# First eight chunks in fp32 on the Sync queue, a hand-ordered prologue, and a rearranged attention step in a fused retention and squared-ReLU kernel

## The chip, the cores and the metric

One core of one Trainium2 chip. The metric is the device time of one execution in microseconds (us). Runs of a kernel are compared with runs of the kernel before on the same chip. Two executions, one in run 8 and one in run 9, were marked slow (over 1.5% above the fastest of the same kernel); medians and ranges below leave them out.

Engine names follow the profile: PE is TensorE (matmul), PEld its weight loads, DVE is VectorE, ACT is ScalarE, POOL is GpSimd, SP is Sync. A name ending in q is that engine's sequencer.

## The reference

```python
# q, k, v: (4, 8, 768, 64) fp32;  w_in: (512, 2048);  w_out: (2048, 512)
gamma = 1 - 2.0 ** (-5 - arange(8));  scale = 1 / sqrt(64)
for t in range(768):
    state = gamma * state + outer(k[t], v[t])       # for each batch and head
    y[t] = scale * q[t] @ state
x = y.transpose(0, 2, 1, 3).reshape(3072, 512)
h = maximum(x @ w_in, 0)
out = (h * h) @ w_out                               # (3072, 512) fp32
```

The kernel cuts the 3072 tokens into 24 chunks of 128 tokens, six to a batch. For each chunk, the attention part scales k, transposes k and q, forms scores under a causal mask, and adds what the running state gives. The feed-forward part (`f1`, `f2`) then runs on blocks of chunks. All matmuls are bf16.

## The kernel before

Parts that the change and the argument touch; `...` marks cuts.

```python
blocks = [[0, 1], [2, 3]]            # then four chunks each
def load_chunk(m):                   # k in fp32 on Sync; q and v cast to bf16 on the way, on POOL
    for name, src, dt in (("kn", k, FP32), ("qs", q, BF16), ("vs", v, BF16)):
        t = ldpool.tile([P, H, D], dt, tag=name, name=f"{name}{m}")
        eng = nc.sync if dt == FP32 else nc.gpsimd
        eng.dma_start(t[:], src[b, :, i * C : (i + 1) * C, :].rearrange("h s d -> s h d"))
def load_w(which, s): ...            # a quarter of w_in or w_out, cast to bf16, on POOL

load_chunk(0)
... # identity, on POOL
load_chunk(1)
... # the constants for the decay factors, on POOL: iota ex_i, causal mask, iota t_i
load_chunk(2); load_chunk(3)
for s in range(NSL): load_w("i", s)

def a_cast(m):  # DVE: ks = k * factor
def a_turn(m):  # PE: 8 transposes;  ACT: PSUM -> kqT
def a_score(m): # PE: 8 matmuls of 64 rows (row tiles);  DVE: mask -> pt
def a_out(m):
    ...
    if i > 0:
        for p in range(NP):
            for hh in range(2):
                r = slice(64 * hh, 64 * hh + 64)
                nc.tensor.matmul(yt[r, p, :], lhsT=s_bf[r, p, :], rhs=kqT[r, 1, p, :], ...)  # 64x64 tiles
    ... # 8 value matmuls (64-column tiles), 8 matmuls for the state c (64-column tiles)
    ... # DVE: xts = yt * yf;  ACT: state copy c -> s
def f1(b, fb):  # 4 matmuls, ACT relu, DVE square
def f2(b, j, part): # 4 matmuls; after the last part ACT copies and Sync stores

a_cast(0); a_turn(0); fill_yf(0, C)
a_cast(1); a_turn(1); a_score(0); fill_yf(C, S)
...
# f1(0) with chunks 2 and 3 between, f1(1), f2(0), f2(1); then each block woven with the
# attention pieces of the next: a_score, a_cast, a_turn and a_out, each a piece of its own
```

Of the kernel before, what the change touches and what calls it, by code (L numbers as in the profile page):

```python
# [18 lines left out]
def kernel(  # L19
# [9 lines left out]
    nc = tc.nc  # L29
# [11 lines left out]
    assert NCB == NP and S % C == 0 and NFB % 4 == 0  # L41
    NSL = 4
    FPS = NFB // NSL
    FW = FPS * P
    scale = 1.0 / float(np.sqrt(D))
    gammas = [1.0 - 2.0 ** (-5.0 - h) for h in range(H)]

    blocks = [[0, 1], [2, 3]]
    while blocks[-1][-1] + 1 < NCHUNK:
        c0 = blocks[-1][-1] + 1  # L50
        blocks.append(list(range(c0, min(c0 + 4, NCHUNK))))
    where = {m: (b, j) for b, ms in enumerate(blocks) for j, m in enumerate(ms)}
# [4 lines left out]
    ldpool = ctx.enter_context(tc.tile_pool(name="ldpool", bufs=7))  # L57
    bfpool = ctx.enter_context(tc.tile_pool(name="bfpool", bufs=4))
    atpool = ctx.enter_context(tc.tile_pool(name="atpool", bufs=3))
    xtpool = ctx.enter_context(tc.tile_pool(name="xtpool", bufs=3))  # L60
    hpool = ctx.enter_context(tc.tile_pool(name="hpool", bufs=2))
# [11 lines left out]
    raw = {}  # L73
    w_in_bf = [const.tile([P, NCB, FW], BF16, name=f"w_in_bf{s}") for s in range(NSL)]
    w_out_bf = [const.tile([P, FPS, DM], BF16, name=f"w_out_bf{s}") for s in range(NSL)]

    def load_chunk(m):
        b, i = divmod(m, NCH)
        got = []
        for name, src, dt in (("kn", k, FP32), ("qs", q, BF16), ("vs", v, BF16)):  # L80
            t = ldpool.tile([P, H, D], dt, tag=name, name=f"{name}{m}")
            eng = nc.sync if dt == FP32 else nc.gpsimd
            eng.dma_start(  # L83
                t[:], src[b, :, i * C : (i + 1) * C, :].rearrange("h s d -> s h d")
            )
            got.append(t)
        raw[m] = got

    def load_w(which, s):
        if which == "i":  # L90
            nc.gpsimd.dma_start(w_in_bf[s][:], w_in_v[:, :, s * FW : (s + 1) * FW])
        else:
            nc.gpsimd.dma_start(w_out_bf[s][:], w_out_v[:, s * FPS : (s + 1) * FPS, :])

    load_chunk(0)


    ident = const.tile([P, P], BF16)
# [10 lines left out]
    load_chunk(1)  # L109

    lng = const.tile([P, H], FP32)
    for h in range(H):
        nc.gpsimd.memset(lng[:, h : h + 1], float(np.log(gammas[h])))
    ex_i = const.tile([P, NCH, H], I32)
    nc.gpsimd.iota(ex_i[:], pattern=[[C, NCH], [0, H]], base=0, channel_multiplier=1)
# [11 lines left out]
    lnp = const.tile([P, NP], FP32)  # L127
    for h in range(H):
        r = slice(64 * (h % 2), 64 * (h % 2) + 64)
        nc.gpsimd.memset(lnp[r, h // 2 : h // 2 + 1], float(np.log(gammas[h])))  # L130
    t_i = const.tile([P, S], I32)
    nc.gpsimd.iota(t_i[:], pattern=[[1, S]], base=0, channel_multiplier=0)

    load_chunk(2)
    load_chunk(3)
    for s in range(NSL):
        load_w("i", s)


    ex_f = const.tile([P, NCH, H], FP32)  # L140
    nc.vector.tensor_copy(ex_f[:], ex_i[:])
    nc.vector.tensor_tensor(
        out=ex_f[:],
        in0=ex_f[:],
# [5 lines left out]
    nc.vector.tensor_scalar_mul(kf[:], kf[:], scale)  # L150
# [3 lines left out]
    yf = const.tile([P, NP, S], FP32)  # L154

    def fill_yf(lo, hi):
        for p in range(NP):
            nc.scalar.activation(  # L158
                yf[:, p, lo:hi], t_f[:, lo:hi], AF.Exp, scale=lnp[:, p : p + 1]
            )  # L160

# [5 lines left out]
    def a_cast(m):  # L167
        i = m % NCH
        kn, qs, vs = raw.pop(m)
        ks = bfpool.tile([P, H, D], BF16, tag="ks", name=f"ks{m}")  # L170
        nc.vector.tensor_tensor(  # L171
            out=ks[:],
            in0=kn[:],
            in1=kf[:, i, :, None].to_broadcast([P, H, D]),
            op=ALU.mult,
        )
        at[m] = dict(ks=ks, qs=qs, vs=vs)

    def a_turn(m):
        a = at[m]  # L180
        tp = ps_tp.tile([P, 2, NP, P], BF16, tag="tp", name=f"tp{m}")
        for j, src in enumerate((a["ks"], a["qs"])):
            for p in range(NP):
                nc.tensor.transpose(tp[:, j, p, :], src[:, 2 * p : 2 * p + 2, :], ident[:])  # L184
        kqT = atpool.tile([P, 2, NP, P], BF16, tag="kqT", name=f"kqT{m}")
        nc.scalar.activation(kqT[:], tp[:], AF.Copy)
        a["kqT"] = kqT
# [24 lines left out]
    def a_out(m):  # L212
        i = m % NCH
        a = at.pop(m)
        ks, vs, kqT, pt = a["ks"], a["vs"], a["kqT"], a["pt"]
        b, j = where[m]
        if j == 0:
            xts[b] = xtpool.tile([P, NP, 4 * P], BF16, tag="xt", name=f"xt{b}")
        yt = ps_yt.tile([P, NP, P], FP32, tag="yt", name=f"yt{m}")
        if i > 0:  # L220
            s_bf = state["s"]
            for p in range(NP):
                for hh in range(2):
                    r = slice(64 * hh, 64 * hh + 64)
                    nc.tensor.matmul(
                        yt[r, p, :],
                        lhsT=s_bf[r, p, :],
                        rhs=kqT[r, 1, p, :],
                        start=(p == 0),
                        stop=False,  # L230
                        skip_group_check=True,
                    )
        for p in range(NP):
            for hh in range(2):
                r = slice(64 * hh, 64 * hh + 64)
                nc.tensor.matmul(
                    yt[r, p, :],
                    lhsT=vs[:, 2 * p + hh, :],
                    rhs=pt[:, hh, p, :],
                    start=(i == 0 and p == 0),  # L240
                    stop=(p == NP - 1),
                    skip_group_check=True,
                )
        if i < NCH - 1:
# [3 lines left out]
            for p in range(NP):  # L248
                for hh in range(2):
                    h = 2 * p + hh  # L250
                    r = slice(64 * hh, 64 * hh + 64)
                    nc.tensor.matmul(  # L252
                        c[r, p, :],
                        lhsT=ks[:, h, :],
                        rhs=vs[:, h, :],
                        start=(i == 0 and p == 0),
                        stop=(p == NP - 1),
                        skip_group_check=True,
                    )
        nc.vector.tensor_tensor(  # L260
            out=xts[b][:, :, j * P : (j + 1) * P],
            in0=yt[:],
            in1=yf[:, :, i * C : (i + 1) * C],
            op=ALU.mult,
        )
        if i < NCH - 1:
            s_new = atpool.tile([P, NP, D], BF16, tag="s", name=f"s{m}")
            nc.scalar.activation(s_new[:], c[:], AF.Copy)
            state["s"] = s_new
# [4 lines left out]
    def f1(b, fb):  # L274
        n = len(blocks[b]) * P
        if fb == 0:
            h2s[b] = hpool.tile([P, NFB, 4 * P], BF16, tag="h2", name=f"h2_{b}")
        h2 = h2s[b]
        hp = ps_f.tile([P, 4 * P], FP32, tag="psf", name=f"hp{b}_{fb}")
        s, r = divmod(fb, FPS)  # L280
        for cb in range(NCB):
# [3 lines left out]
                rhs=xts[b][:, cb, :n],  # L285
# [3 lines left out]
        nc.scalar.activation(h2[:, fb, :n], hp[:, :n], AF.Relu)  # L289
        nc.vector.tensor_mul(h2[:, fb, :n], h2[:, fb, :n], h2[:, fb, :n])  # L290
# [3 lines left out]
    def f2(b, j, part):  # L294
        m = blocks[b][j]
# [3 lines left out]
        for r in range(FPS):  # L299
# [3 lines left out]
                lhsT=h2s[b][:, fb, j * P : (j + 1) * P],  # L303
# [8 lines left out]

    def all_f1(b):
        return [lambda fb=fb: f1(b, fb) for fb in range(NFB)]

    def all_f2(b):
        return [
            lambda j=j, s=s: f2(b, j, s) for j in range(len(blocks[b])) for s in range(NSL)
        ]

    def stages(ms):

        seq = []
        for n in range(len(ms) + 2):
            if 0 <= n - 1 < len(ms):
                seq.append(lambda m=ms[n - 1]: a_score(m))
            if n < len(ms):
                seq.append(lambda m=ms[n]: a_cast(m))
                seq.append(lambda m=ms[n]: a_turn(m))
            if 0 <= n - 2 < len(ms):  # L330
                seq.append(lambda m=ms[n - 2]: a_out(m))
        return seq

    def weave(quanta, side):
        n, done = len(quanta), 0
# [6 lines left out]


    a_cast(0)
    a_turn(0)
    fill_yf(0, C)
    a_cast(1)
    a_turn(1)
    a_score(0)
    fill_yf(C, S)  # L350
    a_cast(2)
    a_turn(2)
    a_out(0)
    a_score(1)
    a_out(1)
    a_cast(3)
    a_score(2)
    a_turn(3)
    load_chunk(4)
    load_w("o", 0)  # L360
    load_chunk(5)
    load_w("o", 1)
    load_chunk(6)
    load_w("o", 2)
    load_chunk(7)
    load_w("o", 3)
    load_chunk(8)

    q0 = all_f1(0)
    side = [lambda: a_out(2), lambda: a_score(3), lambda: a_out(3)]  # L370
    for fb in range(NFB):
        q0[fb]()
        if fb in (1, 3, 6):
            side.pop(0)()
    nxt = 9
    q1 = all_f1(1)
    for x in range(NFB // 2):
        q1[x]()
    weave(q1[NFB // 2 :] + all_f2(0) + all_f2(1), stages(blocks[2]))
    for b in range(2, len(blocks)):  # L380
        while nxt < NCHUNK and nxt <= blocks[b][-1] + 5:
            load_chunk(nxt)
            nxt += 1
        weave(all_f1(b) + all_f2(b), stages(blocks[b + 1]) if b + 1 < len(blocks) else [])
# [30 lines left out]
```

## Time and profile before

| | before |
|---|---|
| median of its first 3 runs | 239.28 us (238.09 to 240.16) |
| profiled run, its span | 237.42 us, 235.7 us |
| PE busy | 214.2 us, 91% |
| first transposes / first feed-forward matmul | 9.55 / 22.68 us |
| block of four chunks in the middle | 34.95 us |
| last block, without attention | 27.66 us |

The Trainium skill ("Trainium Kernel Development and Optimization", Performance Expectations) warns that matmul busy time is a bad measure of distance to the roofline. The argument here therefore goes by starts: the time from the start of one group of matmuls to the start of the next is what that group costs PE.

The page, busy times (us, share of the span, instructions), and two rows of its 40 slices:

```profile
PE 214.2 (91%) x1728; PEld 110.9 (47%) x1728; DVE 101.4 (43%) x188; ACT 109.6 (46%) x190; POOL 51.5 (22%) x82
...
PE   0166997799999999999999999999999999999993
...
PEclk9999999999999999999999999999999999999999
```

PE is full from the fifth slice on, but for a dip near 40 us. The loss is at the start. The view of waits of PE from 0 to 65 us (what waited, for what, us in total, times, longest) tells why:

```profile
PE tp_172 L184 <- DVE ks_170 L171: 9.6, 1, 9.6
PE tp_217 L184 <- DVE ks_215 L171: 1.9, 1, 1.9
...
PE tp_646 L184 <- DVE ks_637 L171: 1.0, 1, 1.0
PE tp_594 L184 <- DVE ks_585 L171: 1.0, 1, 1.0
PE hp_0_348 L282 <- DMA w_in_bf_93<-in_moe_w_in_dram: 0.7, 1, 0.7
...
PE st_612 L196 <- ACT kqT_603 L186: 0.7, 1, 0.7
```

PE stood 9.6 us for the first scaled k. Its data had landed at about 3.5 us. What was missing were the factors, whose first input, `ex_i`, POOL made only after issuing four loads. This is POOL's timeline (start, us, engine, line, operation, out<-in, count):

```profile
1.27 1.01 POOL L83 DMA_DIRECT2D qs_103<-in_q_dram  x1 [0.80 <-POOLq L399]
...
3.69 0.89 POOL L83 DMA_DIRECT2D qs_114<-in_q_dram  x1
...
5.73 0.21 POOL L115 IOTA ex_i<- 128x48 int32 x1
...
11.97 0.79 POOL L91 DMA_DIRECT2D w_in_bf_93<-in_moe_w_in_dram  x1
```

PE's timeline near the first feed-forward, whose groups of four are `hp`:

```profile
22.68 1.03 PE L282 MATMUL hp_0_348<-xt_228,w_in_bf_93 128*128 128x256 bf16 x4 [0.71 <-DMA w_in_bf_93<-in_moe_w_in_dram]
23.51 1.06 PE L282 MATMUL hp_1_355<-xt_228,w_in_bf_93 128*128 128x256 bf16 x4
...
27.11 0.61 PE L282 MATMUL hp_4_416<-xt_228,w_in_bf_94 128*128 128x256 bf16 x4
27.55 0.60 PE L282 MATMUL hp_5_423<-xt_228,w_in_bf_94 128*128 128x256 bf16 x4
```

From 22.68 to 23.51 a group of four takes 0.83 us; from 27.11 to 27.55 the same shape takes 0.44. PE is slow ("cold") until it has been busy for a while, as the Trainium skill ("TensorE: Matmul & The Clock Gate", Part 1) describes. The row PEclk, the clock granted by the throttle, does not show this: the trace's first clock record begins at 25.67 us, and the row counts time without a record as full. The starts show it.

In the middle of the kernel, PE's timeline reads so (`tp` transposes, `st` scores, `yt` L225 state product, `yt` L236 values, `c` the new state):

```profile
105.61 1.03 PE L282 MATMUL hp_6_1422<-xt_1104,w_in_bf_94 128*128 128x512 bf16 x4
106.66 0.40 PE L184 MATMUL tp_1429<-ident,ks_1413 128*128 128x128 bf16 x4
...
107.98 1.03 PE L282 MATMUL hp_8_1447<-xt_1104,w_in_bf_95 128*128 128x512 bf16 x4
108.94 0.40 PE L196 MATMUL st_1454<-kqT_1438 64*128 64x128 bf16 x8
109.27 1.04 PE L282 MATMUL hp_9_1465<-xt_1104,w_in_bf_95 128*128 128x512 bf16 x4
...
127.41 1.03 PE L301 MATMUL op_1641<-w_out_bf_99,h_3_1355 128*128 128x512 bf16 x4
128.37 0.41 PE L225 MATMUL yt_1665<-kqT_1504,s_1632 64*64 64x128 bf16 x8
128.71 0.41 PE L236 MATMUL yt_1665<-pt_1563,vs_1339 128*64 128x128 bf16 x8
128.96 0.29 PE L252 MATMUL c_1530<-vs_1339,ks_1479 128*64 128x64 bf16 x8
129.18 1.04 PE L301 MATMUL op_1641<-w_out_bf_100,h_3_1355 128*128 128x512 bf16 x4
```

The column after the operands tells the part of the array that a matmul uses: 128\*128 is all of it, 64\*128 a row tile, 128\*64 a column tile, 64\*64 both. These are called forms below. A feed-forward group of four takes 0.86 us by itself. It takes 0.96 in front of a score (107.98 to 108.94) or a state product (127.41 to 128.37): entering the tiled form costs 0.10 us. It takes 1.05 in front of these transposes (105.61 to 106.66). No PE wait over the listing's threshold is reported there, but the waits of the weight loads show one:

```profile
PEld L184 <- DVE ks_1413 L171: 0.5, 1, 0.5
```

DVE ended the scaling of that k at 106.61, 0.05 us before the load. Six of the last twelve chunks lose 0.19 us in this way, the other six nothing.

### The profile page before, as it was taken

What the parts mean: (1) busy time and instruction counts of PE and PEld (TensorE: products, weight loads), DVE (VectorE), ACT (ScalarE), POOL (GpSimd) and SP (SyncE); (2) the same over time, 40 slices, a digit from 0 to 9 for tenths busy, and PEclk for the clock granted to TensorE, in tenths of its full rate; (3) what the DMA queues carried; (4) which work ended last, traced back from release to release, by engine and by line L of the source; (5) the groups of instructions that cost most, each with busy time, mean ns of one, the idle gap of its engine ahead of it and who ended that gap; (6) DMA issues with size and microseconds to landing.
All of it is one profiled execution on the core that took longest, in us unless ns stands there. A gap on an engine that the chain in (4) does not pass through costs nothing.

```text
span 235.7 us, 4145 instructions
## 1 busy us (share of the span) xinstructions
PE 214.2 (91%) x1728; PEld 110.9 (47%) x1728; DVE 101.4 (43%) x188; ACT 109.6 (46%) x190; POOL 51.5 (22%) x82
## 2 busy tenths in 40 slices
PE   0166997799999999999999999999999999999993
PEld 0145785454544444444445544444544554444441
DVE  0446665642356533356634266534266524144100
ACT  2292586432277721277722277621377622277221
POOL 8983155642410102410203410100000000000000
PEclk9999999999999999999999999999999999999999
DMA  8999999998994087993078992041170011100112
GB/s 130 215 191 197 198 181 190 185 161 127 138 183 79 3 89 87 111 185 65 4 88 91 112 194 54 2 64 47 46 178 4 0 47 46 63 29 0 42 47 89
DMA packets 82579, 23.34 MB, mean 99 GB/s; under 512 B 75392, under 2 KB 79488, under 8 KB 82560
## 3 DMA queue, kind: packets, MB, share of 16 engines
q0 software_dynamic: 54144, 10.49, 52.7%
q1 hardware_dynamic: 28416, 12.59, 20.3%
q8 instruction: 13, 0.21, 0.4%
q14 instruction: 6, 0.05, 0.1%
HBM read 27.26 MB, written 6.29 MB: 142 GB/s over the span
## 4 chain that ended last, share of the span: by engine, by line
PE 85%; DMA 5%; POOL 4%; DVE 2%; ACT 1%; issue 1%; ACTq 0%; POOLq 0%
DMA w_in_bf_93<-in_moe_w_in_dram 5%; PE op_2057 L301 2%; PE op_1641 L301 2%; PE op_1232 L301 2%; PE op_865 L301 2%; PE op_795 L301 2%; PE op_2470 L301 2%; PE op_2411 L301 2%; PE op_762 L301 2%; PE op_2378 L301 2%; PE op_1549 L301 2%; PE op_1140 L301 2%; PE op_2529 L301 2%; PE op_2008 L301 2%; PE op_1975 L301 2%; PE op_1700 L301 2%
## 5 line engine op out<-in xcount | busy, mean ns | idle before, releaser
L282 PEld LDWEIGHTS <-w_in_bf_93 128*128 128x128 bf16 x112 | 10.6, 101 | 9.6 <-DMA w_in_bf_93<-in_moe_w_in_dram 1.0
L282 PEld LDWEIGHTS <-w_in_bf_95 128*128 128x128 bf16 x112 | 10.5, 98 | 9.3
L282 PEld LDWEIGHTS <-w_in_bf_94 128*128 128x128 bf16 x112 | 10.6, 98 | 8.9
L282 PEld LDWEIGHTS <-w_in_bf_96 128*128 128x128 bf16 x112 | 10.3, 98 | 8.2
L290 DVE TENSOR_TENSOR h_6_2567<-h_6_2567 128x512 bf16<-128x512 bf16 x16 | 6.8, 426 | 10.1 <-ACT h_6_2567 L289 10.1
L290 DVE TENSOR_TENSOR h_5_2177<-h_5_2177 128x512 bf16<-128x512 bf16 x16 | 6.8, 424 | 9.4 <-ACT h_5_2177 L289 9.4
L290 DVE TENSOR_TENSOR h_4_1774<-h_4_1774 128x512 bf16<-128x512 bf16 x16 | 6.8, 424 | 9.4 <-ACT h_4_1774 L289 9.4
L290 DVE TENSOR_TENSOR h_2_939<-h_2_939 128x512 bf16<-128x512 bf16 x16 | 6.8, 423 | 9.4 <-ACT h_2_939 L289 9.4
L290 DVE TENSOR_TENSOR h_3_1355<-h_3_1355 128x512 bf16<-128x512 bf16 x16 | 6.8, 424 | 8.9 <-ACT h_3_1355 L289 8.9
L301 PEld LDWEIGHTS <-h_6_2567 128*128 128x128 bf16 x64 | 6.3, 98 | 7.5
L184 PE MATMUL tp_172<-ident,ks_170 128*128 128x128 bf16 x4 | 0.6, 307 | 9.6 <-DVE ks_170 L171 9.6
L301 PEld LDWEIGHTS <-h_4_1774 128*128 128x128 bf16 x64 | 5.8, 98 | 6.5
L301 PEld LDWEIGHTS <-h_2_939 128*128 128x128 bf16 x64 | 5.8, 98 | 6.5
L301 PEld LDWEIGHTS <-h_5_2177 128*128 128x128 bf16 x64 | 5.8, 98 | 6.5
L301 PEld LDWEIGHTS <-h_3_1355 128*128 128x128 bf16 x64 | 5.8, 98 | 6.5
L290 DVE TENSOR_TENSOR h_1_528<-h_1_528 128x256 bf16<-128x256 bf16 x16 | 4.6, 291 | 4.8 <-ACT h_1_528 L289 3.7
L290 DVE TENSOR_TENSOR h_0_347<-h_0_347 128x256 bf16<-128x256 bf16 x16 | 4.5, 291 | 4.8 <-ACT h_0_347 L289 3.5
L184 PEld LDWEIGHTS <-ks_170 128*128 128x128 bf16 x4 | 0.3, 130 | 9.5 <-DVE ks_170 L171 9.5
L301 PEld LDWEIGHTS <-h_1_528 128*128 128x128 bf16 x32 | 2.8, 98 | 3.1
L158 ACT ACTIVATE yf<-t_f,lnp 128x128 f32<-128x128 f32 (+1 forms) x8 | 4.2, 603 | 0.0
L301 PEld LDWEIGHTS <-h_0_347 128*128 128x128 bf16 x32 | 2.9, 98 | 2.8
L83 POOL DMA_DIRECT2D vs_2173<-in_v_dram x1 | 0.9, 876 | 13.9 <-PE c_1530 L252 13.9
(803 smaller groups left out, 516.5 us busy)
## 6 DMA issues: line engine op xcount, KB each, us to landing
w_in_bf_93<-in_moe_w_in_dram POOLq DMA_DIRECT2D x1, 512.0 KB, 10.7
w_in_bf_94<-in_moe_w_in_dram POOLq DMA_DIRECT2D x1, 512.0 KB, 13.2
w_in_bf_95<-in_moe_w_in_dram POOLq DMA_DIRECT2D x1, 512.0 KB, 15.2
w_in_bf_96<-in_moe_w_in_dram POOLq DMA_DIRECT2D x1, 512.0 KB, 17.1
w_out_bf_97<-in_moe_w_out_dram POOLq DMA_DIRECT2D x1, 512.0 KB, 17.6
w_out_bf_98<-in_moe_w_out_dram POOLq DMA_DIRECT2D x1, 512.0 KB, 13.7
w_out_bf_99<-in_moe_w_out_dram POOLq DMA_DIRECT2D x1, 512.0 KB, 11.8
w_out_bf_100<-in_moe_w_out_dram POOLq DMA_DIRECT2D x1, 512.0 KB, 11.6
```

The costliest lines, as they stand in the source:

```text
L83: eng.dma_start(t[:], src[b, :, i * C : (i + 1) * C, :].rearrange("h s d -> s h d"))
L158: nc.scalar.activation(yf[:, p, lo:hi], t_f[:, lo:hi], AF.Exp, scale=lnp[:, p : p + 1])
L184: nc.tensor.transpose(tp[:, j, p, :], src[:, 2 * p : 2 * p + 2, :], ident[:])
L282: nc.tensor.matmul(hp[:, :n], lhsT=w_in_bf[s][:, cb, r * P : (r + 1) * P], rhs=xts[b][:, cb, :n], start=(cb == 0), stop=(cb == NCB - 1),)
L290: nc.vector.tensor_mul(h2[:, fb, :n], h2[:, fb, :n], h2[:, fb, :n])
L301: nc.tensor.matmul(op[:], lhsT=h2s[b][:, fb, j * P : (j + 1) * P], rhs=w_out_bf[part][:, r, :], start=(fb == 0), stop=(fb == NFB - 1),)
```

## The change

The change's intent: the first eight chunks of q and v come in fp32 on one Sync queue and are cast by engines; the weights are issued between chunks 0 to 3 and chunks 4 to 7; POOL makes constants first; dummy matmuls keep PE warm; the first blocks are ordered by hand; the state product becomes four full-array matmuls on block-diagonal tiles; and the score of the next chunk stands directly behind the value and state matmuls.

```diff
-    blocks = [[0, 1], [2, 3]]  # then fours
+    for n in (2, 2, 1, 3, 4, 4, 4, 4): ...
+    FIRST = 8                                  # fp32 on Sync for q, v of chunks below 8
+    for m in range(4):
+        load(nc.sync, "k", m); load(nc.sync, "q", m); load(nc.sync, "v", m)
     ... # POOL: the two iotas, identity and mask now come before any DMA issue; small memsets on DVE
 def a_cast(m):
-        nc.vector.tensor_tensor(out=ks[:], in0=kn[:], in1=kf..., op=ALU.mult)
+        nc.vector.scalar_tensor_tensor(out=ks[:], in0=kn.pop(m)[:], scalar=scale, in1=kf..., ...)
+        if m < FIRST:
+            if m < 4: nc.scalar.activation(qs[m][:], qn.pop(m)[:], AF.Copy)
+            else:     nc.gpsimd.tensor_copy(qs[m][:], qn.pop(m)[:])
+            nc.gpsimd.tensor_copy(vs[m][:], vn.pop(m)[:])
 def a_out(m, after=None):
-                for hh in range(2): nc.tensor.matmul(yt[r, p, :], lhsT=s_bf[r, p, :], rhs=kqT[r, 1, p, :], ...)
+                nc.tensor.matmul(yt[:, p, :], lhsT=s_bd[i % 2][:, p, :], rhs=kqT[:, 1, p, :], ...)
-            nc.scalar.activation(s_new[:], c[:], AF.Copy)
+            for hh in range(2): nc.scalar.activation(s_bd[(i + 1) % 2][r, :, r], c[r, :, :], AF.Copy)
+        if after is not None: a_score(after)
+def fill(n): # n matmuls of zeros, 512 columns
+run("Y0 Z12 K0 T0 Y1 Z2 K1 S0 Z2 T1 P0 K2 S1 Y2 Z2 T2")     # K cast, T turn, S score, P out,
+load_w_in(0); load_w_in(1)                                   # Y fill_yf, Z fill, F f1, G f2, L load
+run("P1 K3 S2 Y3 Z2 T3 P2 S3 Y4 Z4")
+... # w_in 2, 3; w_out 0..3; chunks 4..7 on Sync, the first behind the landing of w_out 2
+run("F0.0 P3 Y5 F0.1 F0.2 F0.3 F1.0 F1.1 F1.2 F1.3")
+... # then f1 and f2 of chunks 0..3 weight slice by weight slice
+run("K4 G0.3 G1.3 G2.3 K5 T4 G3.0 S4 G3.1 T5 G3.2 P4 S5 G3.3 K6")
+... # block of chunk 4 alone, then chunks 5..7, then fours
+def side(ms): # for each chunk: a_turn(m + 1); cast(m + 2); a_out(m, m + 1)
```

## The prediction

> **What bounds it now.** By the page, TensorE (PE) is 91% busy and 85% of the chain that ended last. From block 2's first matmul (timeline: 64.6 us) to the last block's (204.4) PE never waits: 34.95 us per block of four chunks. The last block, without attention woven in, takes 27.66, so attention costs (34.95 - 27.66)/4 = 1.82 us per chunk. After it come 3.6 us of eviction, store. Of the first 64.6 us, four chunks of feed-forward (27.7 us) and eight of attention (14.6) would fill 42.3; some 22 are lost:
> - PE waits 9.6 us for the first scaled k (waits view); k landed at 3.6, but its factors came from POOL behind four DMA issues (the iota only at 5.73).
> - chunk 3's v lands at 19.4; weights start behind it in the same POOL queue, at half the packets' share; w_in 0 lands at 22.6.
> - PE is slow until about 25.8: four 256-column matmuls take 0.85 us at 22.7 and 0.44 from 27.1. It is the warm-up the Trainium skill ("TensorE: Matmul & The Clock Gate", Part 1) describes; the trace agrees.
> - from 35 to 45 us PE idles 2.9 us, on k scaling and PSUM evictions.
>
> **The change.**
> 1. Twelve fp32 loads on Sync. Alone, 256-byte packets ran at about 920 per us (packet records, 172 to 175 us), so 1.12 us for a tensor: k0 3.6, q0 4.7, v2 12.5, v3 16. That is no more bandwidth (cast loads reach 1,190 packets per us); what is gained is order.
> 2. POOL makes constants first; kf ready near 2.7 us. First transposes at 5.5 rather than 9.55, after dummy matmuls that should warm PE by then.
> 3. w_in 0 and 1 issue after v2's cast (13.4), so w_in 0's packets meet nearly no competition: first packet 16, at 192 per us 2.7 us, landed 20.4; the other slices every 2.7 us, w_out 3 at 39. Attention for chunks 0 to 2 is then done. PE takes 3.5 us a slice over four chunks, slower than slices land, so never waits.
> 4. Loads of chunks 4 to 7 wait for w_out 2 (36.4) and land from 39 to 51, ahead of use.
> 5. Steady state: four full-array state matmuls (about 0.23 us) replace eight tiled ones (0.34); score directly behind value and key-value products saves one mode entry, 0.10 us (feed-forward quartet 0.86 alone, 0.96 before a tiled group). About 0.2 us per chunk.
> 6. Added: casts on ACT and POOL, two state copies rather than one, a one-chunk block whose evictions are tight. 1 to 2 us of stalls.
>
> **Sum.** First feed-forward 2.3 us earlier; the remaining attention moved before it 1.3; warm start 1.9; stalls near 40 us 3; steady state 3.5; minus 1.5 to 2. About 10 us: span near 225.7, time **229.5 us** (225.5 to 233.5). Faster by over 2%: 0.92; same 0.07; slower 0.01.
>
> **Right or wrong.** Right: first feed-forward matmul at 20 to 21 us at full speed; no PE wait over 1 us after; the full blocks at about 34.2 us rather than 34.95; same tail. Wrong: weights landing after 22; PE cold at 20; block period unchanged.
>
> **What could upset it.** POOL casts slow enough to hold the weights' issue; ACT (q cast, yf, transposes' eviction, state copies: about 3.5 us per chunk against 3.4 of loads) pacing the prologue; PE cold again, waiting for w_in 0; switching between column- and row-tiled matmuls costing the same entry.

## More of the kernel before

The experiments ran in four series: 1 to 4 on chip 4, 5 to 8 on chip 6, 9 to 11 on chip 7, 12 on chip 4 again. Only the first series has a control, and the median of the kernel before moved from 238.96 to 240.66 us between series. So where a median is set against the control's from another series, a difference of a microsecond rests on the traces, not on the medians.

In what follows, a quantum is one group of four feed-forward matmuls, and a piece is a part of the attention put between quanta.

## The result

The changed kernel took 227.60 us (median of 4 runs, 227.43 to 227.99) against 239.03 (4 runs of before, 238.09 to 240.16). The ratio is 0.9522, 95% interval 0.9478 to 0.9566: faster. A ratio is the mean time of one kernel's fast runs over that of the other's in the same rounds, so it is not quite the ratio of the medians.

| | predicted | before | after |
|---|---|---|---|
| time, us | 229.5 (225.5 to 233.5) | 239.03 | 227.60 |
| span of the profiled run | 225.7 | 235.7 | 225.9 |
| first transposes | 5.5 | 9.55 | 5.86 |
| v of chunk 2 landed | 12.5 | | 11.9 |
| first feed-forward matmul | 20 to 21 | 22.68 | 19.46 |
| w_out 3 landed | 39 | | 37.6 |
| block of four in the middle (after: the first two) | 34.2 | 34.95 | 33.70, 33.57 |
| PE waits over 1 us after the first feed-forward | none | | 1.2 and 1.3 |

PE's timeline after, at the first feed-forward:

```profile
19.46 0.61 PE L316 MATMUL hp_0_443<-xt_250,w_in_bf_96 128*128 128x256 bf16 x4 [0.24 <-DMA w_in_bf_96<-in_moe_w_in_dram]
...
20.70 0.61 PE L316 MATMUL hp_1_478<-xt_250,w_in_bf_96 128*128 128x256 bf16 x4
21.15 0.60 PE L316 MATMUL hp_2_485<-xt_250,w_in_bf_96 128*128 128x256 bf16 x4
21.58 0.60 PE L316 MATMUL hp_3_492<-xt_250,w_in_bf_96 128*128 128x256 bf16 x4
23.39 0.60 PE L316 MATMUL hp_0_499<-xt_250,w_in_bf_96 128*128 128x256 bf16 x4 [1.20 <-ACT h_0_442 L323]
```

The first groups are already 0.44 us apart: PE is warm. But it then waits 1.2 us for an eviction by ACT. The waits of PE over the whole of the run after:

```profile
PE tp_1119 L217 <- DVE ks_1116 L192: 1.3, 1, 1.3
PE hp_0_499 L316 <- ACT h_0_442 L323: 1.2, 1, 1.2
PE fill L351 <- DVE zero L146: 1.2, 1, 1.2
PE st_339 L227 <- ACT kqT_296 L218: 1.1, 1, 1.1
PE st_392 L227 <- ACT kqT_357 L218: 1.1, 1, 1.1
```

And the middle of the kernel:

```profile
105.48 1.03 PE L316 MATMUL hp_11_1682<-xt_1203,w_in_bf_98 128*128 128x512 bf16 x4
106.35 0.39 PE L253 MATMUL yt_1689<-kqT_1533,s_bd_175 128*128 128x128 bf16 x4
106.67 0.41 PE L264 MATMUL yt_1689<-pt_1619,vs_1363 128*64 128x128 bf16 x8
106.91 0.29 PE L280 MATMUL c_1598<-vs_1363,ks_1511 128*64 128x64 bf16 x8
107.14 0.40 PE L227 MATMUL st_1713<-kqT_1635 64*128 64x128 bf16 x8
107.47 1.04 PE L316 MATMUL hp_12_1724<-xt_1203,w_in_bf_99 128*128 128x512 bf16 x4
```

The feed-forward group ahead takes 0.87 us: the full-array state product costs no entry. It takes 0.32 us itself, because the entry is now paid between it and the tiled values. The change from the column tiles of `c` to the row tiles of `st` costs no more than the change from `c` back to the full array that it replaces: `c` takes 0.223 us in both kernels. But it is not free. The values take 0.248 us with `c`, of the same form, behind them, 0.348 with a score directly behind (at the end of a batch, where there is no `c`) and 0.346 with a feed-forward group. So every change of form costs some 0.1 us, and after makes three a chunk (state to values, `c` to score, score to feed-forward) where before makes five. Summed from start to start over the last twelve chunks (before 99.5 to 204.4 us, after 94.6 to 194.4):

| per occurrence, us | before | after |
|---|---|---|
| state product, with the entry into tiles | 0.341 + 0.094 | 0.316 |
| entry in front of the score | 0.096 | 0 |
| loss in front of the transposes (mean) | 0.094 | 0 |
| transposes / score / values / new state | 0.452 / 0.330 / 0.264 / 0.223 | 0.447 / 0.329 / 0.264 / 0.223 |

Where the 9.8 us of span came from, in three stretches of PE's timeline. After reaches the first block of chunks 8 to 11 with two groups of transposes and one of scores already done that before still had to do (2 x 0.447 + 0.329 = 1.22 us); they are credited to the second stretch.

| stretch | before | after | gained |
|---|---|---|---|
| start to first feed-forward matmul | 22.68 | 19.46 | 3.2 |
| from there to the block of chunks 8 to 11 | 76.87 | 75.17 | 1.7 + 1.2 |
| from there to the end | 136.1 | 131.2 | 4.9 - 1.2 |

### The profile page after: what moved, and what is told of

Same layout as the page of the kernel before. It is cut to its first block, busy times and chain, and to the rows that moved or that the text cites. A ratio compares the mean times of both kernels' runs of the same rounds, so it can differ in the third digit from the quotient of the medians.

```text
span 225.9 us, 4271 instructions
## 1 busy us (share of the span) xinstructions
PE 212.3 (94%) x1736; PEld 117.5 (52%) x1736; DVE 103.2 (46%) x221; ACT 123.1 (54%) x246; POOL 43.5 (19%) x62
## 4 chain that ended last, share of the span: by engine, by line
PE 84%; DMA 5%; ACT 4%; SPq 3%; DVE 2%; issue 1%; POOL 0%; ACTq 0%
DMA w_in_bf_96<-in_moe_w_in_dram 3%; SPq L91 3%; DMA vn_120<-in_v_dram 2%; PE op_2633 L335 2%; PE op_1480 L335 2%; PE op_2223 L335 2%; PE op_2512 L335 2%; PE op_2317 L335 2%; PE op_1920 L335 2%; PE op_1826 L335 2%; PE op_1427 L335 2%; PE op_1072 L335 2%; PE op_2860 L335 2%; PE op_705 L335 2%; PE op_695 L335 2%; PE op_2820 L335 2%
## 5 line engine op out<-in xcount | busy, mean ns | idle before, releaser
L316 PEld LDWEIGHTS <-w_in_bf_96 128*128 128x128 bf16 x128 | 11.4, 98 | 10.3 <-issue 1.4
L316 PEld LDWEIGHTS <-w_in_bf_98 128*128 128x128 bf16 x128 | 11.8, 98 | 8.7
L316 PEld LDWEIGHTS <-w_in_bf_99 128*128 128x128 bf16 x128 | 11.6, 98 | 8.2
L316 PEld LDWEIGHTS <-w_in_bf_97 128*128 128x128 bf16 x128 | 11.4, 98 | 8.1
L324 DVE TENSOR_TENSOR h_5_2687<-h_5_2687 128x512 bf16<-128x512 bf16 x16 | 6.8, 426 | 11.8 <-ACT h_5_2687 L323 11.8
L324 DVE TENSOR_TENSOR h_2_1544<-h_2_1544 128x512 bf16<-128x512 bf16 x16 | 6.8, 424 | 10.7 <-ACT h_2_1544 L323 10.6
L324 DVE TENSOR_TENSOR h_4_2348<-h_4_2348 128x512 bf16<-128x512 bf16 x16 | 6.8, 425 | 9.6 <-ACT h_4_2348 L323 9.6
L324 DVE TENSOR_TENSOR h_3_1951<-h_3_1951 128x512 bf16<-128x512 bf16 x16 | 6.8, 423 | 9.5 <-ACT h_3_1951 L323 9.5
L324 DVE TENSOR_TENSOR h_1_876<-h_1_876 128x128 bf16<-128x128 bf16 (+1 forms) x32 | 8.2, 287 | 4.5 <-ACT h_1_876 L323 4.4
L335 PEld LDWEIGHTS <-h_5_2687 128*128 128x128 bf16 x64 | 6.3, 98 | 7.6
L335 PEld LDWEIGHTS <-h_3_1951 128*128 128x128 bf16 x64 | 6.0, 98 | 7.1
L335 PEld LDWEIGHTS <-h_2_1544 128*128 128x128 bf16 x64 | 6.0, 98 | 7.1
L335 PEld LDWEIGHTS <-h_4_2348 128*128 128x128 bf16 x64 | 5.9, 97 | 6.9
L335 PEld LDWEIGHTS <-h_1_876 128*128 128x128 bf16 x64 | 6.0, 98 | 6.8
L335 PEld LDWEIGHTS <-h_0_442 128*128 128x128 bf16 x64 | 6.0, 98 | 6.6
L351 PE MATMUL fill<-zero 128*128 128x512 bf16 x24 | 8.3, 484 | 1.2 <-DVE zero L146 1.2
L344 ACT ACTIVATE osb_744<-op_695 128x512 f32<-128x512 f32 x1 | 0.6, 597 | 8.2 <-PE op_695 L335 8.2
L253 PEld LDWEIGHTS <-s_bd_175 128*128 128x128 bf16 x48 | 3.6, 98 | 2.3
L351 PEld LDWEIGHTS <-zero 128*128 128x128 bf16 x24 | 2.4, 119 | 4.6 <-issue 2.7
L206 POOL CAST qs_736<-qn_420 128x512 bf16<-128x512 f32 x1 | 0.6, 613 | 19.6 <-DMA qn_420<-in_q_dram 19.6
L235 DVE TENSOR_TENSOR pt_792<-st_783,cmask 128x1024 bf16<-128x1024 f32 x1 | 1.2, 1225 | 5.8 <-PE st_783 L227 5.8
## 6 DMA issues: line engine op xcount, KB each, us to landing
w_out_bf_102<-in_moe_w_out_dram POOLq DMA_DIRECT2D x1, 512.0 KB, 16.6
```

What stands on the lines that cost most here:

```text
L206: nc.gpsimd.tensor_copy(qs[m][:], qn.pop(m)[:])
L235: nc.vector.tensor_tensor(out=pt[:], in0=st[:], in1=cmask[:, None, None, :].to_broadcast([P, 2, NP, P]), op=ALU.mult,)
L253: nc.tensor.matmul(yt[:, p, :], lhsT=s_bd[i % 2][:, p, :], rhs=kqT[:, 1, p, :], start=(p == 0), stop=False, skip_group_check=True,)
L316: nc.tensor.matmul(hp[:, :n], lhsT=w_in_bf[s][:, cb, r * P : (r + 1) * P], rhs=xts[g][:, cb, cols], start=(cb == 0), stop=(cb == NCB - 1),)
L324: nc.vector.tensor_mul(h2[:, fb, cols], h2[:, fb, cols], h2[:, fb, cols])
L335: nc.tensor.matmul(op[:], lhsT=h2s[g][:, fb, j * P : (j + 1) * P], rhs=w_out_bf[part][:, r, :], start=(fb == 0), stop=(fb == NFB - 1),)
```

## The experiments

Two numbers go with each run besides its time. F is the start of the first feed-forward matmul in its profile; it moves from run to run with the landing of the first weights (19.36 to 20.85 us among the runs with the same loads and dummies). B is the time from F to the first feed-forward matmul of the block of chunks 8 to 11, which is free of that; both are read from PE's timeline. After has F 19.46 and B 75.17.

### 1. Control

> The changed kernel as it is, on the chip of this series: 227 to 228 us, span near 225.9, ratio to the kernel before near 0.952. The other runs of the series are read against it.

No edit. 227.59 us (227.47 to 228.24), ratio 0.949 (0.944 to 0.954), span 225.7, F 19.36, B 75.17. As expected. PE had gone cold in this execution by 17 us (a score took 0.61 us) and was warm again by 19.36: the trace's clock records grant half from 15.0 to 18.4 us. That it warmed was not the work of the last dummies, which start only at 18.71.

### 2. Without the dummy matmuls

```diff
-        for _ in range(n):
+        for _ in range(0):
             nc.tensor.matmul(t[:], lhsT=zero[:, :P], rhs=zero[:], ...)
```

> The dummy matmuls left out. Theory (they keep PE warm): PE runs slowly through the prologue and the first feed-forward quartets are 0.85 us apart rather than 0.44 until some 3 us after the first; 1.5 to 3.5 us slower than the control. Rival (they only fill idle time, since loads and ScalarE pace the prologue): within 0.5 us of the control.

228.51 us (227.70 to 229.50), ratio 0.9537 (0.9474 to 0.96), span 225.9, F 18.58, B 76.12. The intervals of this run and the control overlap. PE was cold, as the theory said: 0.83 us from the first group to the next. But B grew by 0.95 us alone, less than the theory's least. Part of it is in PE's own waits: the wait for ACT at 23 us shrank from 1.2 us to 0.7, because PE came there later. Neither expectation holds as written; run 12 takes it up.

### 3. Casting loads again

```diff
-    FIRST = 8
+    FIRST = 0
-    for m in range(4): load(nc.sync, "k", m); load(nc.sync, "q", m); load(nc.sync, "v", m)
+    for m in range(4): load(nc.sync, "k", m)
     ... # POOL constants
+    for m in range(4): load(nc.gpsimd, "q", m); load(nc.gpsimd, "v", m)
-            ins = load(nc.sync, name, m)               # chunks 4 to 7
+            ins = load(nc.sync if name == "k" else nc.gpsimd, name, m)
```

> q and v of the first eight chunks again as casting loads on POOL's queue, issued behind the constants; no casts on engines; all else as changed. Theory (order is what the loads gained, not fp32 on Sync): all twelve early tensors landed by about 15.5 us, the first weight slice by 17 to 19.5, time between 2 us faster and 1 us slower than the control. Rival (fp32 on one Sync queue is what buys the start): the first weights land after 22 and it is over 3 us slower.

229.37 us (229.05 to 229.89), ratio 0.9561 (0.951 to 0.9612), span 227.3, F 20.90, B 75.17: 1.8 us slower, so outside my range and short of the rival's. What I said of the data was right in direction: the first weight slice landed at 16.6 us, 2.8 earlier than in the changed kernel. But PE did not use it. PE's timeline of this run, and the clock row of its page:

```profile
5.93 0.39 PE L218 MATMUL tp<-ident,ks 128*128 128x128 bf16 x4
8.07 0.40 PE L218 MATMUL tp<-ident,qs 128*128 128x128 bf16 x4 [1.76 <-DMA qs<-in_q_dram]
...
10.96 0.63 PE L218 MATMUL tp<-ident,ks 128*128 128x128 bf16 x4
...
20.90 0.60 PE L317 MATMUL hp<-xt,w_in_bf 128*128 128x256 bf16 x4
...
PEclk9769999999999999999999999999999999999999
```

q of chunk 0 arrives 3.3 us later than the 4.7 us of the fp32 load; PE goes cold (0.63 us where 0.39 is warm; the clock records grant half from 9.0 to 15.8 us), and the fixed order of the prologue puts everything behind that. So the Sync queue buys the early first chunk, and pays with later weights.

### 4. Tiled state product

```diff
-                nc.tensor.matmul(yt[:, p, :], lhsT=s_bd[i % 2][:, p, :], rhs=kqT[:, 1, p, :], ...)
+                for hh in range(2):
+                    r = slice(64 * hh, 64 * hh + 64)
+                    nc.tensor.matmul(yt[r, p, :], lhsT=s_bd[i % 2][r, p, r], rhs=kqT[r, 1, p, :], ...)
```

> The state product again as eight 64x64 tiled matmuls, reading the diagonal blocks of the same tiles. Theory: 17 such groups stand where PE has no slack, each 0.12 us longer (0.34 against 0.22): 1.5 to 2.6 us slower than the control, block period up by 0.4 to 0.5 us. Rival (the saving per chunk comes from the entry into tiled mode, which only moves here from the value products to the state products): under 0.5 us slower.

229.88 us (229.23 to 231.67), ratio 0.9592 (0.9529 to 0.9655), span 228.0, F 19.59, B 76.00. 2.3 us slower than the control in the median and in the span, inside the range; the rival falls. The rival had the entry only move from the values to the state product. But the step from the 64x64 form to the values' column tiles costs again: 0.146 us from the last state matmul to the values, 0.056 between pairs inside the group. So this kernel makes one change of form more. From the block of chunks 8 to 11 to the end it took 132.4 us against 131.2 of the control: ten groups at 0.12.

### 5. Score apart from the values

```diff
-            seq.append(lambda m=m: a_out(m, m + 1 if m + 1 < NCHUNK else None))
+            seq.append(lambda m=m: a_out(m))
+            if m + 1 < NCHUNK:
+                seq.append(lambda m=m: a_score(m + 1))
```

> In the last three woven blocks the score of the next chunk is a piece of its own again, not directly behind the value products. Theory (each entry of the tiled form behind full-array matmuls costs PE 0.10 us, a change from column to row tiles nothing): eleven more entries, 1.1 us slower than the control's 227.6 (0.7 to 1.5). Rival (column to row costs the same entry, so adjacency saves nothing): within 0.3 us.

229.09 us (228.62 to 229.32), ratio 0.9586 (0.9553 to 0.9619), span 227.3, F 19.73, B 75.17. The entry in front of the score is back in the timeline, 0.096 us eleven times, and from the block of chunks 8 to 11 to the end it took 132.4 us, 1.2 more than the control. The median is 1.5 us up, at the edge of the range (it is from another chip than the control); 0.3 of that is a later F in the profiled run. The rival falls in what it forecast, but not in its premise: a change from column to row tiles does cost the same (see the values above). The score behind `c` saves because three changes of form become two.

### 6. k scaled directly ahead of its transposes

```diff
     ... # K13 taken out of the block before
-                seq.append(lambda m=m: a_turn(m + 1))
-            if m + 2 < NCHUNK:
-                seq.append(lambda m=m: cast(m + 2))
+                seq.append(lambda m=m: (cast(m + 1), a_turn(m + 1)))
```

> In the same blocks k is scaled directly ahead of the transposes that read it, as in the kernel before, not one chunk earlier. Theory (the lead of the scaling is the part of the steady gain that the prediction left out: before, weight loads of the transposes waited 0.5 us for VectorE and PE lost 0.1 to 0.2 us each time): eleven times that, 1.1 to 2 us slower than the control. Rival (the steady gain is state and adjacency alone): within 0.4 us.

238.84 us (238.49 to 239.97), ratio 1.0006 (0.9969 to 1.0042), span 236.9: all that the change had gained is gone. Both expectations missed, mine by a factor of six. Waits of PE in this run:

```profile
PE tp L217 <- DVE ks L192: 10.9, 7, 1.8
```

With no quantum of feed-forward between the scaling and the transposes, PE waits up to 1.8 us for DVE, which comes to the scaling only behind the square of the quantum before: in one chunk ACT's relu starts at 102.11, the square at 102.74, the scaling at 103.08, the transposes at 103.82. The 11.2 us over eleven chunks are 1.0 us each in the mean; in the trace six chunks lose 1.0 to 1.9 us and five nothing. I had taken the kernel before for this case. It was not: there the scaling stood two quanta ahead. The edit also issues the loads one chunk later, but no DVE wait for a DMA shows after 85 us, so that is not the cause.

### 7. Tables later

```diff
-    run("P1 K3 S2 Y3 Z2 T3 P2 S3 Y4 Z4")
+    run("P1 K3 S2 Y3 Z2 T3 P2 S3 Z4")
-    run("F0.0 P3 Y5 F0.1 ...")
+    run("F0.0 P3 F0.1 ...")
-    run(" ".join(f"G{m}.{s}" ...))
+    run("Y4 Y5 " + " ".join(f"G{m}.{s}" ...))
```

> The tables of chunk positions 4 and 5 are computed behind the first feed-forward, where ScalarE is idle, not in front of its evictions. Theory (the 1.2 us wait of PE at 22.2 us is ScalarE's table work ahead of three evictions, with only three PSUM buffers): 0.9 to 1.4 us faster than the control. Rival (weight slice 1, landed near 22, would hold PE in its place): under 0.4 us.

226.51 us (225.97 to 227.26), ratio 0.9479 (0.9441 to 0.9518), span 225.2, F 20.00, B 73.97: 1.1 us faster than the control in the median and exactly the 1.2 us in B. PE's timeline has no wait left between the first groups; they run in one piece (the view ends at 30 us). The intervals of this run's ratio and the control's overlap, so the gain rests on B:

```profile
21.23 8.99 PE L316 MATMUL hp<-xt,w_in_bf 128*128 128x256 bf16 x80
```

### 8. And a new seam behind the one-chunk block

```diff
-    weave(all_f1(2) + all_f2(2), [... "P5", "T6", "S6", "K7 L8", "P6", "T7", "S7 L9"])
-    run("P7")
-    weave(all_f1(3) + all_f2(3), "K8 T8 K9,S8 L10,T9 K10,...")
+    at2 = {0: "P5", 2: "T6", 5: "S6", 8: "K7 L8", 10: "P6", 13: "T7", 16: "S7 L9", 18: "K8 P7 T8 K9"}
+    for x, f in enumerate(all_f1(2) + all_f2(2)): run(at2.get(x, "")); f()
+    weave(all_f1(3) + all_f2(3), "S8 L10,T9 K10,...")
```

> The same, and at the seam behind the one-chunk block: k of chunk 8 is scaled ahead of chunk 7's output, and its transposes stand between output products rather than behind them. Theory: the 1.3 us wait at 65 us goes too, so 2.0 to 2.7 us faster than the control, near 225.2. Rival (PE then waits for chunk 7's output or chunk 8's transposed eviction instead): no better than the run before.

Five fast runs from 226.52 to 229.58 us, median 227.66 (the sixth, 230.33, was slow), ratio 0.9533 (0.9484 to 0.9582); span of the profiled run 224.7, F 19.89, B 73.65. Even the fastest run, 226.52, is short of the 225.2 hoped for, and the runs scatter more than any before. The expectation failed. The granted clock does not explain it: it was 0.993 in the run of 229.58 us, but also 0.992 in the fastest run of after (227.43) and 0.99 in one of run 10's fast ones (225.66). In the trace, k of chunks 8 and 9 is fetched in 256-byte packets on Sync next to casting loads on POOL, and DVE now meets those k sooner, while work behind them waits (in run 11 the mask of chunk 0 starts at 8.99 us, behind the late k of chunk 1, though its scores were done by 7.7).

### 9. Scaling one piece ahead

```diff
     ... # K13 taken out of the block before
-                seq.append(lambda m=m: a_turn(m + 1))
-            if m + 2 < NCHUNK:
-                seq.append(lambda m=m: cast(m + 2))
+                seq.append(lambda m=m: cast(m + 1))
+                seq.append(lambda m=m: a_turn(m + 1))
-        while loaded[0] + 1 < NCHUNK and loaded[0] < m + 2:
+        while loaded[0] + 1 < NCHUNK and loaded[0] < m + 3:
```

> k is scaled as a piece of its own directly ahead of the piece with its transposes, so usually one feed-forward quantum earlier, as the kernel before had it; loads are issued as early as in the control, which the late scaling of the run before had also changed. Theory (the lead decides how long PE waits, loads do not): 0.1 to 0.2 us for each of eleven chunks, 1.0 to 2.2 us over the control's 227.6, far from the 238.8 of no lead. Rival (the later loads made the run before slow): within 0.5 us of the control.

228.73 us (227.67 to 229.14; a sixth run, 231.58, was slow), ratio 0.9536 (0.9491 to 0.9582), span 227.2. The median lies in my range, but not for my reason: in the trace the loss in front of the transposes is zero, and the profiled run owes its length to F at 20.85 us, where the weights came 1.4 us late. From the block of chunks 8 to 11 to the end it took 131.6 us, of which 0.45 are transposes that the control had done before; that leaves the control's 131.2. So my expectation missed. Pieces stand 2.7 quanta apart here, two in the kernel before. The three cases line up as a lead of 0, 2 and 2.7 quanta costing 1.0, 0.1 and 0 us a chunk in the mean, but a kernel with a lead of exactly two was not run, so the 0.1 is read off before alone.

### 10. New seam with earlier loads

```diff
-    run("K4 G0.3 G1.3 G2.3 K5 T4 ...")
+    run("K4 L8 G0.3 G1.3 G2.3 K5 L9 T4 ...")
     ... # late tables and the seam of run 8; loads of chunks 10 to 15 two places earlier
```

> The late tables and the new seam, with the loads of chunks 8 and 9 issued about ten us earlier. Theory (the new seam was uneven from run to run because VectorE, in order, waits for k of chunks 8 and 9 that arrive in a crowd of casting loads): the runs agree within 1.5 us and stand at 224.8 to 225.8. Rival (the unevenness has another cause): again a spread of over 2 us, or no faster than the late tables alone at 226.5.

225.80 us (225.28 to 226.83), ratio 0.9422 (0.9376 to 0.9467), span 224.6, F 20.34, B 73.04. The runs agree within 1.6 us (1.5 was expected) and the median is at the edge of the range, so the rival falls on the scatter. That it is faster than run 7 rests on B (73.04 against 73.97), since the intervals of the two ratios overlap. B is 2.1 us below the control's. This version beats both kernels. That DVE's wait for k was what made run 8 uneven fits this, but no slow run of it was profiled, so that cause is inferred.

### 11. fp32 on Sync for two chunks only

```diff
-    FIRST = 8
+    FIRST = 2
     ... # on top of run 7: q, v of chunks 2 and 3 as casting loads behind the constants,
     ... # those of chunks 4 to 7 as casting loads behind the weights
```

> On top of the late tables: fp32 on Sync for q and v of chunks 0 and 1 alone; q and v of chunks 2 to 7 as casting loads on POOL, the first four issued behind the constants, the weights after v1's cast. Theory (fp32 on Sync buys the early arrival of the first chunk; the casting loads carry the rest with less engine time): first weight slice landed by 16.5 to 18.5, first feed-forward at 17.5 to 19 as ScalarE and PE allow, 0.5 to 2 us faster than the late tables alone (226.5). Rival (all of the first four chunks need the Sync queue): slower than 226.5.

229.84 us (229.06 to 230.62), ratio 0.9588 (0.9546 to 0.9629), span 228.3, F 22.88, B 73.96: 3.3 us slower than run 7, all of it ahead of F. The theory falls. POOL's waits:

```profile
POOL vs L211 <- DMA vn<-in_v_dram: 6.9, 1, 6.9
```

The two kinds of load now share the DMA engines. By the packet records, 256-byte packets on Sync fell from about 1,000 per us (after, 2 to 14 us) to 300 to 450 (6 to 12 us), beside about 550 to 660 of the casting kind. v of chunk 1 arrived so late that POOL could cast it only at 14.13 us instead of 8.86, and the weights were issued behind that cast, at 14.69 rather than 12.47. Yet the weights did not hold PE: their first slice landed at 20.2 us, much as in run 7 (20.0), and no wait of PE for it is listed. The attention ahead of them did: k of chunk 2 could be scaled only at 15.15 us (10.60 in run 7), q of chunk 1 cast only at 10.90 (8.47), and PE was cold, its granted clock half from 11.0 to 21.2 us.

### 12. The fastest version without the dummies

```diff
     ... # run 10, and
-        for _ in range(n):
+        for _ in range(0):
```

> The fastest version of this series (late tables, new seam, earlier loads of chunks 8 and 9: 225.8 us) without the dummy matmuls. Theory (a warm PE is worth its 1.9 us only where nothing else makes PE wait just behind; in the changed kernel the wait for ScalarE's tables at 22 us swallowed most of it, which is why leaving the dummies out there cost 0.2 us of span): 1.2 to 2.2 us slower than 225.8. Rival (loads and weights set the pace there, so the dummies buy nothing in any version): under 0.6 us.

226.94 us (226.03 to 227.68), ratio 0.9473 (0.9438 to 0.9508), span 225.3, F 19.12, B 74.96. B is 1.92 us above run 10, twice the 0.95 that the dummies were worth in the changed kernel; the time is 1.1 us longer, just short of the range, with the rival further off. B says that the dummies are worth what was predicted for a warm start once nothing else makes PE wait behind it. The time pays less, because F came earlier in both runs without dummies (18.58 and 19.12, against 19.36 and more with them). In both, the first weights were issued no earlier than elsewhere (12.75 and 12.74 us) but landed 5.8 and 6.3 us later, against 5.9 to 7.4 in the runs with dummies and the same loads. Whether the dummies have to do with that, two profiles can't tell.

## Why the prediction was right, and where its steps were not

- **Total and span: right.** 9.8 us of span against "about 10 us". The time was predicted 1.9 us too high. The predicted time lies 3.8 us over the predicted span, about as the median of before lies over its profiled span (239.28 over 235.65); but after's device time exceeds its span by 1.7 us, and so does that of before's profiled run (237.42 over 235.7). That profiled run of before was a quick one: the other four executions were 0.7 to 2.7 us longer, and within the span, since time less span is 1.7 to 1.8 us in the experiments' executions of before too. So the time fell by more (11.4 us) than the profiled spans did. No trace shows where those microseconds lie.
- **Start: right.** "First feed-forward 2.3 us earlier" was 3.2, at full speed. Sync packets ran at about 1,000 per us, not 920; k and q of chunk 0 landed as predicted (3.6 and 4.7), and from v of chunk 2 on the landings were 0.6 to 1.4 us earlier.
- **"What is gained is order", not the queue: half right.** Run 3 shows the trade: casting loads bring the weights 2.8 us sooner and the first chunk 3.3 us later, and lose 1.8. Run 11 shows that mixing the two kinds early is worse than either.
- **"Remaining attention moved 1.3": done as said.** Before still ran the output of chunk 2 (24.50 to 25.80 us) and the score of chunk 3 (26.78 to 27.11) behind its first feed-forward; in after both are over by then. Since before ran the output cold, this gain overlaps with the next.
- **"Warm start 1.9": right of PE's own time, wrong of its worth in this kernel.** Leaving the dummies out cost 0.95 us of B; with the wait behind it removed, 1.92. Against before it is less: before was cold until 25.7, and its groups from 22.68 to 25.80 took 1.3 us more than they take warm.
- **"Stalls near 40 us 3 ... minus 1.5 to 2": this step failed.** The old stalls went, but from the first feed-forward on after has waits of 4.1 us of its own (1.2 for ACT's tables, 1.3 at the seam, the rest for transposed k and q and masked scores in and around the one-chunk block). The item "no PE wait over 1 us" was wrong twice. Runs 7 and 10 remove these two and gain 1.1 and 1.8 us.
- **Steady state: mechanism right, size low.** Predicted 0.2 us a chunk; over the last twelve chunks it is (136.10 - 131.23 - 1.22)/12 = 0.30. The state product (0.12, run 4) and the entry (0.10, run 5) were of the size said. But the state product did not shrink from 0.34 to 0.23: it takes 0.32, and what falls away is the entry ahead of it, a change of form. And the change between column and row tiles, named as a risk, does cost the same; it did no harm because it replaces another. A third term was left out: the scaling of k now runs further ahead of the transposes, and their loss of 0.09 a chunk is gone. That before's loss is a wait for the scaling is read in its trace (0.05 us between the two); how exactly the lead sets it is read from traces (runs 6 and 9), not from one clean pair.
- So the total was met because errors cancelled. For the second stretch I had counted 1.3 + 1.9 + 3 less 1.5 to 2, some 4.5 us, besides the steady gain. It measured 2.9 with the work done ahead, and if its eight chunks gained 0.30 each as the later ones do (an assumption, and a generous one: the scores of chunks 4, 6 and 7 are pieces of their own), only 0.5 is left: about 4 us too much. By starts (an estimate from the timelines: what a group takes less what it takes undisturbed, without changes of form) the new waits cost 4.8 us rather than the 4.1 listed, 3.1 more than counted. The cold PE had cost before 0.6 less than counted, the old stalls 0.6 more (3.6). So some 3 of the 4 us are found; the rest stays open. Against it stand the start (0.9 us better) and the steady gain (20 chunks at 0.30, under the same assumption, 2.5 us more than the 3.5 counted).

The Trainium skill ("TensorE: Matmul & The Clock Gate", Part 3, The mechanism) says that a weight load overlaps matmuls in flight only when its row group differs. The trace does not bear this out as it stands: in after, the first weight load of the state product starts 0.21 us ahead of its matmul (106.14 and 106.35), while a feed-forward matmul is in flight on the same rows. What the trace shows instead goes by form: where the form changes, the weight load starts with its matmul (106.66 and 106.67 for the values, 107.13 and 107.14 for the score behind `c`), and there the 0.10 us is lost.

## What to carry to other kernels

Cost a group of matmuls from its start to the next start, and look at what stands in front: the entry into tiled matmuls, and a producer that is a little too late, were not listed as waits of PE and came to two thirds of the steady gain. The waits of the weight loads listed the second. Count the changes of form and put tiled groups of either kind next to each other, and issue the scaling that feeds PE more than two quanta ahead. At the start of a kernel, count what the new order will make PE wait for next, because a wait removed can be taken up by the one behind it, as in run 2.

## What the Trainium skill lacked or had wrong

- "TensorEngine Tiling (Array Packing)", Key Properties: it says that a change of tiling mode drains TensorE, but no page gives the time. Here 0.094 to 0.096 us from full array to 64-row or 64-column tiles, and as much between column and row tiles and on the way back (values: 0.248 us ahead of the same form, 0.348 ahead of row tiles, 0.346 ahead of full array).
- "TensorE: Matmul & The Clock Gate", Part 3, The mechanism: that a weight load overlaps matmuls only in another row group. Full-array loads start 0.21 us ahead of their matmuls, under a matmul on the same rows.
- The same page, Part 1: it calls the clock events of a trace unreliable, but not that a trace can lack them at its start. In before the first record is at 25.67 us, so PEclk reads 1.00 at 22 to 25 us while groups take 0.83 us rather than 0.44. Later cold stretches are recorded and agree with the starts (run 3: 0.50 from 9.0 to 15.8 us, 0.63 us where 0.39 is warm).
- "DMA: Bandwidth & Descriptors", Anatomy of one DMA: the fit 2.0 us + bytes / 436 GB/s gives 4.4 us for the 1 MiB that the first weight slice reads (an estimate from that page). It landed 7.0 us after its issue began, with next to no other traffic ahead of it; the closing packets of the sixteen engines came between 17.0 and 19.1 us.
- The same page, Specifications: a first byte after about 1 us for loads from GpSimd. The first packet of the weights started 1.6 us after the issue began (12.47 and 14.07), while Sync's packets were still running, so an idle queue may be quicker.
- "GPSIMD Engine Reference", 3.1: it gives 1.8 cycles an element as the best case of a tight loop (768 ns for 512 elements), beside a bound of 1.03 for the shortest bodies, and no figure for a cast. The cast of 128x512 from fp32 to bf16 took 613 ns here, between the two.
